# The last 64 inner MLP channels with tokens on partitions, and GpSimd yielding the shared SBUF port

## Chip, cores and metric

One core of a Trainium2 chip. The metric is the device time of one execution in microseconds (us); medians are over the runs of one kernel.

In the profile's lines PE is TensorE's matmul and PEld its weight load, DVE is VectorE, ACT ScalarE, POOL GpSimd, SP the engine that issues DMAs (a q after a name is its sequencer); L963 is line 963 of that run's kernel, so the numbers shift from run to run. SBUF is the memory that the engines work on, PSUM the one in banks into which matmuls sum.

## The reference, cut to what matters

```python
def _A_ref(x, k_cache, v_cache, wq, wo):       # attention: 32 heads of 128, 2048 queries, 2048 keys
    q = (x @ wq) ...; p = softmax(q @ k^T * Dh ** -0.5)
    return (p @ v) ... @ wo

def _B_ref(x, w1, w2, w3, w4):                 # x: 2048 tokens x 640
    h = gelu(layernorm(x) @ w1)
    hs = (four column groups of h, each shifted by +1, -1, +2, -2 tokens) @ w2
    x1 = x + hs
    h2 = gelu(layernorm(x1) @ w3) @ w4         # w3: 640 x 1728, w4: 1728 x 640
    return x1 + h2

h = layernorm(x) * (1 + ca) + sa;  x = x + ga * _A_ref(h, ...)
h = layernorm(x) * (1 + cb) + sb;  x = x + gb * _B_ref(h, ...)
```

1728 inner channels are 13 x 128 + 64. The change is about those last 64.

## The kernel before

The program is a list of operations with predicted durations; a scheduler written in Python places them in time and so fixes each engine's order of instructions, which the chip then follows with semaphores. After about 1195 us of attention comes the MLP. It works on four chunks of 512 tokens: stage A is w1, B is w2, **C the up projection (w3)**, **D the down projection (w4)**. In C channels lie on partitions: the weights are a 128x128 block of w3, the moving side is 512 tokens. The last block has 64 channels and 64 zero columns.

```python
def w3_part(ch, key):
    for f in range(NF):                        # NF = 14 blocks of 128 channels
        m = Tile(pool="T")
        for kk in range(KT):                   # KT = 5
            P.op("PE", lambda e, ...: e.matmul(m.ap, w3_ap[:, kk, f * 128:(f + 1) * 128], nT_ap[ch][:, kk, :],
                                               start=(kk == 0), stop=(kk == KT - 1)), MM(QC), ...)
        P.op("ACT", lambda e, ...: e.activation(gT_ap[:, f, :], m.ap, GELU), ...)

def w4_tile(t, key):                           # one tile of 128 tokens, two halves of 320 outputs
    ...
    for n, (mm, o, c0, c1) in enumerate(parts):
        for f in range(NF):
            P.op("PE", lambda e, ...: e.matmul(mm[:, o:o + c1 - c0], gT_ap[:, f, i * 128:(i + 1) * 128],
                                               w4_ap[f][:, c0:c1], start=(f == 0), stop=(f == NF - 1)), ...)

P.op("POOL", lambda e: e.memset(w3_ap[:, :, FF:FP], 0.0), ...)          # the zero columns
P.op("DVE", lambda e: e.memset(w4_ap[NF - 1][FL:128, :], 0.0), ...)     # and zero rows
```

The other half concerns VectorE and GpSimd. The scheduler assumes that some operations of the two ("dual": two inputs in SBUF) use a port that they share (the prediction gives the page and the traces for it), and lets neither start, in its plan, before the other's has ended. The durations it plans with are estimates:

```python
COST = {"POOL": (1600, 950), "DVE": (825, 590)}
...
x = port["POOL" if e == "DVE" else "DVE"] if o.dual else 0.0
st.append((max(r, t_eng[e], x), o.prio, o.seq, o))
...
if o.dual:
    port[e] = s + o.dur                        # planned time; no semaphore comes of it
```

Nothing makes the chip keep to the plan: if an engine is some hundred nanoseconds off, both instructions are issued at the same time after all.

Of the kernel before, what the change touches and what calls it, by code (L numbers as in the profile page):

```python
# [6 lines left out]
ACT = mybir.ActivationFunctionType  # L7
# [33 lines left out]
class Plan:  # L41
# [50 lines left out]
    def schedule(self):  # L92
# [18 lines left out]
        pe = sorted((o for o in self.ops if o.eng == "PE"), key=lambda o: (o.prio, o.seq))  # L111
        pe_i = 0
        port = {"POOL": 0.0, "DVE": 0.0}
        while len(self.all) < len(self.ops):
            best = None
            for e in self.ENG:
# [18 lines left out]
            s, o = best[0], best[3]  # L135
            e = o.eng
# [3 lines left out]
            for t in o.newps:  # L140
                b = min(free[t.pool])
# [3 lines left out]
                    o.deps.setdefault(d, False)  # L145
            o.start = s
            if o.dual:
                port[e] = s + o.dur
            t_eng[e] = s + (o.dur if o.dma or e == "PE" else max(o.dur - self.LAP.get(e, 0.0), 60.0))
            self.busy[e] += o.dur  # L150
# [129 lines left out]
def fast_path(nc, es, flag, A_x, A_k_cache, A_v_cache, A_wq, A_wo, B_w1, B_w2, B_w3, B_w4, c, w_mod, out):  # L280
    _, SQ, D = A_x.shape
    _, H, SK, DH = A_k_cache.shape
    FF = B_w3.shape[1]
    assert (SQ, D, H, SK, DH) == (2048, 640, 32, 2048, 128) and FF == 1728
    KT, NKT, HD, QC, NC = D // 128, SK // 128, D // 2, 512, SQ // 512
    NF = (FF + 127) // 128
    FL = FF - (NF - 1) * 128
    FP = NF * 128
    G4 = D // 4
    HG = 4  # L290
    NG = H // HG
# [66 lines left out]
    OT = [[T() for _ in range(4)] for _ in range(2)]  # L358
    gT_ap = OO_t[:, 0:NF * QC].rearrange("p (f q) -> p f q", f=NF)
    gT = [T() for _ in range(NF)]  # L360
    wq = [[T() for _ in range(HG)] for _ in range(2)]
    wo = [T() for _ in range(2)]
    hT = [[T() for _ in range(KT)] for _ in range(NC)]
# [12 lines left out]
    tmp = [T(t[:]) for t in tmp_t]  # L376
    rl = T(rl_t[:])
    ident, ones = T(ident_t[:]), T(ones_t[:])
    W3_OFF = 2 * KVW
    w3_ap = KV_t[:, W3_OFF:W3_OFF + KT * FP].rearrange("p (k n) -> p k n", k=KT)  # L380
    w3 = [T() for _ in range(KT)]
    W4_HI = W3_OFF + KT * FP
    NW4 = 12
    w4_ap = [KV_t[:, f * D:(f + 1) * D] for f in range(NW4)] + [KV_t[:, W4_HI + f * D:W4_HI + (f + 1) * D] for f in range(NF - NW4)]
    w4 = [T() for _ in range(3)]
    w4_of = lambda f: w4[0] if f < 6 else (w4[1] if f < NW4 else w4[2])
    assert NW4 * D <= W3_OFF and W4_HI + (NF - NW4) * D <= NKV * KVW

    MM = lambda n: n / 2.4 + 2.5
    dve = lambda n, psum=False: (n + (150 if psum else 145)) / 0.96  # L390
# [5 lines left out]
    def dma(eng, fn, kb, reads, writes, prio, need=(), after=(), over=()):  # L396
        return P.op(eng, fn, {"SP": 480, "ACT": 480, "POOL": 1000}[eng], reads, writes, prio, dma=True, kb=kb, need=need, after=after, over=over)

    def dmaT(fn, kb, reads, writes, prio, need=(), over=()):
        return P.op("SP", fn, 1270, reads, writes, prio, dma=True, kb=1.63 * kb, need=need, over=over)  # L400
# [131 lines left out]
                                              op0=ALU.subtract, op1=ALU.mult),  # L532
             445, src_t + (mvs[g][i], rs[g]), (dst_t,), prio, after=after)

    COST = {"POOL": (1600, 950), "DVE": (825, 590)}

    def tt(eng, out, a, b, op, rd, wr, prio):
        P.op(eng, lambda e: e.tensor_tensor(out=out, in0=a, in1=b, op=op), COST[eng][0], rd, wr, prio, lat=300 if eng == "POOL" else None, dual=True)  # L538
# [368 lines left out]
    for g in range(4):  # L907
        dma("SP", lambda e, g=g: e.dma_start(w_half[1][g * 32:(g + 1) * 32, 4, :], w2_rows[128:G4, g, :]), 40, (), (w2b[g],), E, over=tuple(wT[1]))
    kv = lambda *i: tuple(t for b in i for t in K[b] + [V[b]])
    for k, old in ((0, kv(2)), (1, kv(2)), (2, kv(2, 3)), (3, kv(3)), (4, kv(3, 4))):  # L910
        dma("SP", lambda e, k=k: e.dma_start(w3_ap[:, k, 0:FF], B_w3[k * 128:(k + 1) * 128, :]), 432, (), (w3[k],), E + 5 + k, over=old)
    for i, (f0, f1, old) in enumerate(((0, 6, kv(0)), (6, 12, kv(0, 1)))):
        dma("SP", lambda e, f0=f0, f1=f1: e.dma_start(KV_t[:, f0 * D:f1 * D].rearrange("p (f n) -> p f n", n=D),
                                                      B_w4[f0 * 128:f1 * 128, :].rearrange("(f p) n -> p f n", p=128)),
            960, (), (w4[i],), E + 11 + i, after=last_ot if i else (), over=old)
    dma("SP", lambda e: e.dma_start(w4_ap[NF - 2], B_w4[(NF - 2) * 128:(NF - 1) * 128, :]), 160, (), (w4[2],), E + 10, over=kv(4))
    w4b = T()
    dma("SP", lambda e: e.dma_start(w4_ap[NF - 1][0:FL, :], B_w4[(NF - 1) * 128:FF, :]), 80, (), (w4b,), E + 10, over=kv(4))

    pad, pad2 = T(), T()  # L920
    P.op("POOL", lambda e: e.memset(w3_ap[:, :, FF:FP], 0.0), 300, (), (pad,), E + 12, over=kv(2, 3, 4))
    P.op("DVE", lambda e: e.memset(w4_ap[NF - 1][FL:128, :], 0.0), 400, (), (pad2,), E + 12, slack=500.0, over=kv(4))


    DEL = [1, -1, 2, -2]
# [57 lines left out]
                    tt("DVE", v.ap, v.ap, x1[u].ap, ALU.add, (v, x1[u]), (v,), key + 100)  # L983

    def w3_part(ch, key):
        for f in range(NF):
            m = Tile(pool="T")
            for kk in range(KT):
                P.op("PE", lambda e, m=m, f=f, kk=kk: e.matmul(m.ap, w3_ap[:, kk, f * 128:(f + 1) * 128], nT_ap[ch][:, kk, :],  # L989
                                                                    start=(kk == 0), stop=(kk == KT - 1)),  # L990
                     MM(QC), (w3[kk], pad) + tuple(nT[ch]), (m,), key + f + 0.1 * kk, accum=True)
            P.op("ACT", lambda e, m=m, f=f: e.activation(gT_ap[:, f, :], m.ap, GELU),  # L992
                 act(QC), (m,), (gT[f],), key + f, over=tuple(a for b in On + OT for a in b) if ch == 0 else ())

    def w4_tile(t, key):
        i = t % 4
        b = xb[t]
        m = Tile(pool="W")
        last = t == SQ // 128 - 1
        if last:  # L1000

            m3 = Tile(pool="T")
            parts = ((m, 0, 0, HD), (m, 512, HD, 512), (m3, 0, 512, D))
        else:
            parts = ((m, 0, 0, HD), (m, 512, HD, D))
        for n, (mm, o, c0, c1) in enumerate(parts):
            for f in range(NF):
                P.op("PE", lambda e, f=f, mm=mm, o=o, c0=c0, c1=c1: e.matmul(mm[:, o:o + c1 - c0], gT_ap[:, f, i * 128:(i + 1) * 128],  # L1008
                                                                             w4_ap[f][:, c0:c1], start=(f == 0), stop=(f == NF - 1)),
                     MM(c1 - c0), (gT[f], w4_of(f), w4b, pad2), (mm,), key + n + 0.01 * f, accum=True)  # L1010
            if last:
                w, o_ = tmp[t % 2], xin[(0, 3, 1)[n]]
                P.op("DVE", lambda e, mm=mm, o=o, c0=c0, c1=c1: e.tensor_tensor(out=w[:, c0:c1], in0=mm[:, o:o + c1 - c0], in1=mod_t[5][:, c0:c1], op=ALU.mult),
                     dve(c1 - c0), (mm,) + tuple(mod[5]), (w,), key - 1000)
                P.op("DVE", lambda e, o_=o_, c0=c0, c1=c1: e.tensor_tensor(out=o_[:, c0:c1], in0=w[:, c0:c1], in1=b[:, c0:c1], op=ALU.add),
                     dve(c1 - c0), (w, b), (o_,), key)
                dma("SP", lambda e, o_=o_, c0=c0, c1=c1: e.dma_start(out2d[t * 128:(t + 1) * 128, c0:c1], o_[:, c0:c1]), 80, (o_,), (), key)
        if last:
            return
        o_ = xin[t % 4]  # L1020
        if t < SQ // 128 - 2:
            P.op("DVE", lambda e: e.tensor_tensor(out=two(b.ap), in0=wide(m), in1=two(b.ap), op=ALU.add), 825, (m, b), (b,), key - 1000)
            tt("DVE", b.ap, b.ap, mod_t[5][:], ALU.mult, (b,) + tuple(mod[5]), (b,), key)
            tt("DVE", o_.ap, b.ap, x1[t].ap, ALU.add, (b, x1[t]), (o_,), key)
        else:
            w = tmp[t % 2]
            P.op("DVE", lambda e: e.tensor_tensor(out=two(w.ap), in0=wide(m), in1=two(mod_t[5][:]), op=ALU.mult), 825, (m,) + tuple(mod[5]), (w,), key - 1000)
            tt("DVE", o_.ap, w.ap, b.ap, ALU.add, (w, b), (o_,), key)
        dma("SP", lambda e: e.dma_start(out2d[t * 128:(t + 1) * 128, :], o_.ap), 160, (o_,), (), key)
# [770 lines left out]
```

## Time and profile before

| | before |
|---|---|
| median (range) of 3 runs | 1369.59 us (1368.27 to 1372.08) |
| profiled span | 1367.0 us |
| TensorE holes, 50 to 1167 us | none |
| TensorE holes, 1167 to 1200 us | 2.04 us |
| TensorE holes, 1200 us to the end | none |

A hole is what the distance of one matmul's start to the next exceeds columns/2.4 + 2.6 ns by; how that pace was read from the chain is told in the prediction. Some matmuls have no record; a gap that is one missing matmul (216 ns at 512 columns) is not counted. Busy time by stretch (the end of attention with the first layer norms of the MLP; stages A and B with the first C; the rest). The columns are the stretch, its length, then each engine's busy us with the count of instructions, clock, DMA share and GB/s:

```profile
core 0: us, PE busy (x) PEld busy (x) DVE busy (x) ACT busy (x) POOL busy (x), PEclk, DMA share, GB/s
1165.00:1200.00 35.00, 34.17 (x318) 22.60 (x321) 29.41 (x86) 27.93 (x37) 18.46 (x17) 1.00 0.43 113
1200.00:1262.00 62.00, 61.45 (x368) 36.34 (x372) 58.22 (x168) 19.89 (x33) 0.00 (x0) 1.00 0.26 61
1262.00:1367.00 105.00, 101.53 (x632) 61.28 (x635) 50.93 (x116) 30.68 (x50) 0.00 (x0) 1.00 0.15 39
```

In the first stretch VectorE and GpSimd are both at work (29.4 and 18.5 of 35 us): of these three, only there can the port matter. Afterwards GpSimd does nothing. Now the chain over the first chunk's C, by start, length, instruction and count (L963 is B, L989 is C):

```profile
1223.52 1.36 PE f_M L963 x10
1224.88 0.05 issue
1224.93 1.03 PE f_S L989 x4
...
1238.91 1.08 PE f_O L989 x5
1239.98 1.36 PE f_S L963 x10
```

C runs from 1224.88 to 1239.98: 15.10 us for 70 matmuls, one after the other. (The 0.05 us called issue, with x4 after it, is a matmul without a record.) The place where the two engines meet is shown by two instructions on record in the prediction, at 1176.04 (GpSimd) and 1176.39 (VectorE, 1.88 us instead of some 0.88). What follows there, start and length first, with the idle time before it in brackets:

```profile
1178.19 0.48 DVE L771 TENSOR_TENSOR f_tmp<-f_M,f_mod 128x320 f32<-128x320 f32 x1
...
1180.08 1.54 POOL L538 TENSOR_TENSOR f_hT<-f_tmp,f_y 128x640 bf16<-128x640 f32 x1 [1.01 <-DVE f_rl L832]
```

L771 empties a PSUM bank that TensorE needs next; VectorE comes to it 1.0 us late, which here nothing yet waits for. GpSimd's next instruction, a memset, starts at 1178.71.

### The profile page before, as it was taken

The numbers are of one execution on the slowest core, as the hardware profiler recorded it, in microseconds if no ns is written. First come the engines' busy times: TensorE is split into PE (matmuls) and PEld (weight loads), VectorE is DVE, ScalarE is ACT, GpSimd is POOL, SyncE is SP. The second block draws the span as 40 slices with busy tenths as digits, with TensorE's granted clock in tenths as the row PEclk, the third lists the DMA queues.
The fourth block names the chain that finished last, engine by engine and source line by source line (L and its number), as shares of the span: only waits on it lengthen the run. The fifth ranks groups of instructions, "written<-read, shape, count | busy, mean of one in ns | idle before, by whom it ended". The sixth has DMA issues, their size and how long they took to land.

```text
span 1367.0 us, 29510 instructions
## 1 busy us (share of the span) xinstructions
PE 1348.4 (99%) x12778; PEld 934.7 (68%) x13012; DVE 574.7 (42%) x1442; ACT 1102.6 (81%) x1145; POOL 111.5 (8%) x97
## 2 busy tenths in 40 slices
PE   9999999999999999999999999999999999999999
PEld 5677677677667767767776766776776676655665
DVE  5554344544332332333233233233323345798553
ACT  6998888888888888888888888888888888833222
POOL 1000000000000000000000000000233337500000
PEclk9999999999999999999999999999999999999999
DMA  9742624172415221341305121522236000431110
GB/s 217 150 86 51 118 28 80 37 134 48 108 37 94 51 47 36 55 90 28 55 13 99 34 47 35 94 51 48 55 65 140 22 16 19 113 84 47 41 40 31
DMA packets 264932, 90.38 MB, mean 66 GB/s; under 512 B 245065, under 2 KB 262410, under 8 KB 264794
## 3 DMA queue, kind: packets, MB, share of 16 engines
q1 hardware_dynamic: 260826, 84.17, 30.5%
q0 software_dynamic: 672, 2.56, 0.8%
q8 instruction: 104, 1.70, 0.5%
q10 hardware_dynamic: 3296, 1.67, 0.5%
q14 instruction: 34, 0.28, 0.1%
HBM read 41.68 MB, written 2.63 MB: 32 GB/s over the span
## 4 chain that ended last, share of the span: by engine, by line
PE 97%; issue 1%; DMA 1%; DVE 1%; ACT 0%; SPq 0%; DVEq 0%
PE f_O L825 35%; PE f_S L806 29%; PE f_M L729 10%; PE f_M L760 10%; PE f_M L1008 2%; PE f_O L989 2%; PE f_S L989 2%; PE f_S L1008 2%; PE f_S L940 1%; PE f_S L963 1%; PE f_M L963 1%; PE f_O L940 1%; DMA f_W<-in_w_mod_dram 0%; DMA f_hT<-f_xn 0%; PE f_S L760 0%
## 5 line engine op out<-in xcount | busy, mean ns | idle before, releaser
L808 ACT ACTIVATE f_PQ<-f_S 128x1024 bf16<-128x1024 f32 x1024 | 1042.0, 1023 | 136.5 <-PE f_S L806 103.9
L825 PEld LDWEIGHTS f_O<-f_KV,f_PQ 128*128 128x128 bf16 x8192 | 634.9, 98 | 261.3 <-DVE f_OO L834 0.2
L825 PE MATMUL f_O<-f_KV,f_PQ 128*128 128x129 bf16 x8192 | 796.4, 220 | 8.3
L806 PE MATMUL f_S<-f_PQ,f_KV 128*128 128x512 bf16 x1831 | 650.8, 379 | 2.6 <-ACT f_PQ L808 0.5
L768 DVE TENSOR_TENSOR f_y<-f_M,f_y 128x320 f32<-128x320 f32 x192 | 94.4, 492 | 465.6 <-PE f_M L760 465.6
L760 PE MATMUL f_M<-f_wo,f_OO 128*128 128x320 bf16 x992 | 272.9, 299 | 0.0
L806 PEld LDWEIGHTS f_S<-f_PQ,f_KV 128*128 128x128 bf16 x2048 | 191.6, 98 | 13.3 <-ACT f_PQ L808 1.7
L729 PE MATMUL f_M<-f_hT,f_wq 128*128 128x512 bf16 (+1 forms) x635 | 189.1, 378 | 1.9 <-DVE f_tmp L771 0.2
L760 PEld LDWEIGHTS f_M<-f_wo,f_OO 128*128 128x128 bf16 x992 | 96.3, 98 | 28.5
L834 DVE TENSOR_TENSOR f_OO<-f_O,f_rl 128x256 bf16<-128x256 f32 x256 | 108.4, 423 | 8.3
L538 POOL TENSOR_TENSOR f_y<-f_y,f_mod 128x640 f32<-128x640 f32 x32 | 49.1, 1542 | 735.5 <-DVE f_y L768 735.4
L733 DVE CAST f_PQ<-f_M 128x512 bf16<-128x512 f32 x127 | 87.9, 692 | 49.9 <-PE f_M L729 49.6
L729 PEld LDWEIGHTS f_M<-f_hT,f_wq 128*128 128x128 bf16 x640 | 62.5, 98 | 50.6 <-DVE f_hT L595 0.8
L832 DVE RECIPROCAL f_rl<-f_O 128x2 f32<-128x2 f32 x256 | 43.6, 170 | 65.7 <-PE f_O L825 54.8
L992 ACT ACTIVATE f_OO<-f_S 128x512 bf16<-128x512 f32 x28 | 16.7, 597 | 43.6 <-PE f_S L989 43.6
L766 DVE COPY f_y<-f_M 128x320 f32<-128x320 f32 x32 | 15.7, 492 | 57.1 <-PE f_M L760 57.1
L499 DVE BATCH_NORM_STATS2 f_small<-f_y 128x6 f32<-128x320 f32 (+1 forms) x72 | 32.3, 481 | 2.5 <-DMA f_y<-in_A_x_dram 1.5
L1008 PE MATMUL f_M<-f_KV,f_OO 128*128 128x320 bf16 x224 | 31.7, 299 | 0.0
L1008 PE MATMUL f_S<-f_KV,f_OO 128*128 128x320 bf16 (+1 forms) x224 | 31.0, 296 | 0.0
L544 ACT ACTIVATE f_xn<-f_y,f_small 128x640 bf16<-128x640 f32 x10 | 9.1, 915 | 26.3 <-DVE f_small L523 21.2
L661 DVE TENSOR_REDUCE f_small<-f_tmp 128x1 f32<-128x640 f32 x20 | 16.4, 820 | 30.1 <-ACT f_PQ L808 30.1
L1008 PEld LDWEIGHTS f_M<-f_KV,f_OO 128*128 128x128 bf16 x224 | 21.9, 98 | 8.9
(151 smaller groups left out, 523.6 us busy)
## 6 DMA issues: line engine op xcount, KB each, us to landing
f_KV<-in_A_v_cache_dram SPq DMA_DIRECT2D x28, 512.0 KB, 5.0
f_wo<-in_A_wo_dram SPq DMA_DIRECT2D x8, 640.0 KB, 4.2
f_wq<-in_A_wq_dram SPq DMA_DIRECT2D x7, 640.0 KB, 4.5
f_xin<-in_A_x_dram SPq DMA_DIRECT2D x13, 320.0 KB, 3.4
out_dram<-f_xin SPq DMA_DIRECT2D x15, 160.0 KB, 1.8
f_KV<-in_B_w_dram SPq DMA_DIRECT2D x5, 432.0 KB, 3.8
f_KV<-in_A_k_cache_dram SPq DMA_TRANSPOSE x128, 2.8
f_OO<-f_OO SPq DMA_TRANSPOSE x128, 2.5
```

Source lines behind the costliest of these rows:

```text
L538: P.op(eng, lambda e: e.tensor_tensor(out=out, in0=a, in1=b, op=op), COST[eng][0], rd, wr, prio, lat=300 if eng == "POOL" else None, dual= ...
L729: P.op("PE", lambda e, i=i, kk=kk, mm=mm, a=a, z=z: e.matmul(mm[:, 0:z - a], wq_t[g % 2][:, kk, hh * 128:(hh + 1) * 128], hT_t[ch][:, kk, ...
L733: P.op("DVE", lambda e: e.tensor_copy(q.ap, m.ap), 690, (m,), (q,), s * NP - 90)
L760: P.op("PE", lambda e, m=m, qt=qt, hf=hf, hh=hh: e.matmul(m[:, 0:HD], OT_ap[gs][:, qt, hh, :], wo_t[g % 2][:, hh, hf * HD:(hf + 1) * HD], ...
L768: P.op("DVE", lambda e, m=m, yt=yt: e.tensor_tensor(out=yt.ap, in0=m[:, 0:HD], in1=yt.ap, op=ALU.add), 490, (m, yt), (yt,), s * NP - 60)
L806: P.op("PE", lambda e, sp=sp, r=r, kt=kt: e.matmul(sp[:, r * QC:(r + 1) * QC], K_ap[b][:, kt * 128:(kt + 1) * 128], q.ap, start=True, stop ...
L808: x = P.op("ACT", lambda e, sp=sp, pt=pt: e.activation(pt.ap.rearrange("p k q -> p (k q)"), sp.ap, ACT.Exp, scale=SCALE), 1021, (sp,), (pt ...
L825: ins = e.matmul(o[bk][:, w * 129:w * 129 + 129], pt[:, r, qt * 128:(qt + 1) * 128], V_ap[b][:, u, 0:129], start=(u == 0 and w == 0), stop ...
L832: P.op("DVE", lambda e, ov=ov, i0=i0: e.reciprocal(rl_t[:, i0:i0 + 2].unsqueeze(2), ov[:, 0:258].rearrange("p (u d) -> p u d", u=2)[:, :, ...
L834: evac.append(P.op("DVE", lambda e, ov=ov, i0=i0, bk=bk: e.tensor_tensor(out=On_ap[gs][:, 2 * bk:2 * bk + 2, hh, :], in0=ov[:, 0:258].rear ...
L989: P.op("PE", lambda e, m=m, f=f, kk=kk: e.matmul(m.ap, w3_ap[:, kk, f * 128:(f + 1) * 128], nT_ap[ch][:, kk, :], start=(kk == 0), stop=(kk ...
L1008: P.op("PE", lambda e, f=f, mm=mm, o=o, c0=c0, c1=c1: e.matmul(mm[:, o:o + c1 - c0], gT_ap[:, f, i * 128:(i + 1) * 128], w4_ap[f][:, c0:c1 ...
```

## The change

**Narrow tile.** For the last 64 channels the operands change places: the tokens become the weights (4 blocks of 128 tokens), the 64 columns of w3 the moving side. That is 20 short matmuls instead of 5 long ones. The result has tokens on partitions and is turned by a DMA transpose for the down projection. Two token blocks share one turned block, so the down projection uses w4's last 64 rows in an upper and a lower copy, the other half zero. A GpSimd memset of these two copies, near 1047 us, takes the place of the two memsets of before (GpSimd's at 1178.71, VectorE's at 1180.20). The narrow group is the first of its chunk.

**Port.** The scheduler gives GpSimd a real dependency (a semaphore wait) on VectorE's last dual operation where its plan has the two close together, and it plans GpSimd with shorter durations.

```diff
             if o.dual:
+                if e == "DVE":
+                    last_dual = o
+                elif last_dual is not None and s < port["DVE"] + 400.0:
+                    o.deps.setdefault(last_dual, False)
                 port[e] = s + o.dur
...
-    COST = {"POOL": (1600, 950), "DVE": (825, 590)}
+    COST = {"POOL": (1502, 858), "DVE": (825, 590)}
...
-    dma("SP", lambda e: e.dma_start(w4_ap[NF - 1][0:FL, :], B_w4[(NF - 1) * 128:FF, :]), 80, (), (w4b,), E + 10, over=kv(4))
-    P.op("POOL", lambda e: e.memset(w3_ap[:, :, FF:FP], 0.0), 300, (), (pad,), E + 12, over=kv(2, 3, 4))
-    P.op("DVE", lambda e: e.memset(w4_ap[NF - 1][FL:128, :], 0.0), 400, (), (pad2,), E + 12, slack=500.0, over=kv(4))
+    P.op("POOL", lambda e: e.memset(KV_t[:, W4Z:W4Z + 2 * D], 0.0), 1400, (), w4b, E, over=kv(2))
+    for i in range(2):
+        dma("SP", lambda e, i=i: e.dma_start(w4_ap[FN + i][i * FL:(i + 1) * FL, :], B_w4[FN * 128:FF, :]), 80, (), (w4b[i],), E + 10)
...  (w3_part; FN = 13, FL = 64)
+        m = Tile(pool="T")
+        for kk in range(KT):
+            for i in range(4):
+                c0 = (i % 2) * 128 + (i // 2) * FL
+                P.op("PE", lambda e, ...: e.matmul(m[:, c0:c0 + FL], nT_ap[ch][:, kk, i * 128:(i + 1) * 128], w3_ap[:, kk, FN * 128:FF],
+                                                   start=(kk == 0 and i == 0), stop=(kk == KT - 1), skip_group_check=True),
+                     MM(FL) + 4, (w3[kk], nT[ch][i]), (m,), key + 0.1 * kk + 0.01 * i, accum=True)
+        P.op("ACT", lambda e, m=m: e.activation(gl_ap, m[:, 0:256], GELU), ...)
+        dmaT(lambda e: e.dma_start_transpose(gT_ap[:, FN, 0:256].rearrange("p (k q) -> p k q", k=2), gl_ap), ...)
-        for f in range(NF):
+        for f in range(FN):
...  (w4_tile)
-   e.matmul(..., gT_ap[:, f, i * 128:(i + 1) * 128], w4_ap[f][:, c0:c1], ...)
+   e.matmul(..., gT_ap[:, f, (i % 2 if f == FN else i) * 128:][:, 0:128], w4_ap[f + i // 2 if f == FN else f][:, c0:c1], ...)
```

More of the change, by code (lines that the diff above doesn't have):

```diff
@@ L113, in schedule @@
         port = {"POOL": 0.0, "DVE": 0.0}
+        last_dual = None
         while len(self.all) < len(self.ops):
@@ L287, in fast_path @@
     FL = FF - (NF - 1) * 128
-    FP = NF * 128
+    FN = NF - 1
     G4 = D // 4
@@ L360, in fast_path @@
     gT = [T() for _ in range(NF)]
+    gl_ap = gT_ap[:, NF - 1, 256:512]
+    gl = T()
     wq = [[T() for _ in range(HG)] for _ in range(2)]
@@ L378, in fast_path @@
     ident, ones = T(ident_t[:]), T(ones_t[:])
-    W3_OFF = 2 * KVW
-    w3_ap = KV_t[:, W3_OFF:W3_OFF + KT * FP].rearrange("p (k n) -> p k n", k=KT)
+    W4Z = 2 * KVW
+    W3_OFF = W4Z + 2 * D
+    w3_ap = KV_t[:, W3_OFF:W3_OFF + KT * FF].rearrange("p (k n) -> p k n", k=KT)
     w3 = [T() for _ in range(KT)]
-    W4_HI = W3_OFF + KT * FP
+    W4_HI = W3_OFF + KT * FF
     NW4 = 12
-    w4_ap = [KV_t[:, f * D:(f + 1) * D] for f in range(NW4)] + [KV_t[:, W4_HI + f * D:W4_HI + (f + 1) * D] for f in range(NF - NW4)]
+    w4_ap = [KV_t[:, f * D:(f + 1) * D] for f in range(NW4)] + [KV_t[:, W4_HI + f * D:W4_HI + (f + 1) * D] for f in range(FN - NW4)] + [KV_t[:, W4Z + i * D:W4Z + (i + 1) * D] for i in range(2)]
     w4 = [T() for _ in range(3)]
     w4_of = lambda f: w4[0] if f < 6 else (w4[1] if f < NW4 else w4[2])
-    assert NW4 * D <= W3_OFF and W4_HI + (NF - NW4) * D <= NKV * KVW
+    assert NW4 * D <= W4Z and W4_HI + (FN - NW4) * D <= NKV * KVW and FL == 64
     MM = lambda n: n / 2.4 + 2.5
@@ L909, in fast_path @@
     kv = lambda *i: tuple(t for b in i for t in K[b] + [V[b]])
-    for k, old in ((0, kv(2)), (1, kv(2)), (2, kv(2, 3)), (3, kv(3)), (4, kv(3, 4))):
-        dma("SP", lambda e, k=k: e.dma_start(w3_ap[:, k, 0:FF], B_w3[k * 128:(k + 1) * 128, :]), 432, (), (w3[k],), E + 5 + k, over=old)
+    for k, old in ((0, kv(2)), (1, kv(2, 3)), (2, kv(3)), (3, kv(3, 4)), (4, kv(4))):
+        dma("SP", lambda e, k=k: e.dma_start(w3_ap[:, k, :], B_w3[k * 128:(k + 1) * 128, :]), 432, (), (w3[k],), E + 5 + k, over=old)
     for i, (f0, f1, old) in enumerate(((0, 6, kv(0)), (6, 12, kv(0, 1)))):
@@ L916, in fast_path @@
     dma("SP", lambda e: e.dma_start(w4_ap[NF - 2], B_w4[(NF - 2) * 128:(NF - 1) * 128, :]), 160, (), (w4[2],), E + 10, over=kv(4))
-    w4b = T()
-    dma("SP", lambda e: e.dma_start(w4_ap[NF - 1][0:FL, :], B_w4[(NF - 1) * 128:FF, :]), 80, (), (w4b,), E + 10, over=kv(4))
-    pad, pad2 = T(), T()
-    P.op("POOL", lambda e: e.memset(w3_ap[:, :, FF:FP], 0.0), 300, (), (pad,), E + 12, over=kv(2, 3, 4))
-    P.op("DVE", lambda e: e.memset(w4_ap[NF - 1][FL:128, :], 0.0), 400, (), (pad2,), E + 12, slack=500.0, over=kv(4))
+    w4b = T(), T()
+    P.op("POOL", lambda e: e.memset(KV_t[:, W4Z:W4Z + 2 * D], 0.0), 1400, (), w4b, E, over=kv(2))
+    for i in range(2):
+        dma("SP", lambda e, i=i: e.dma_start(w4_ap[FN + i][i * FL:(i + 1) * FL, :], B_w4[FN * 128:FF, :]), 80, (), (w4b[i],), E + 10)
     DEL = [1, -1, 2, -2]
@@ L985, in w3_part @@
     def w3_part(ch, key):
-        for f in range(NF):
+        old = tuple(a for b in On + OT for a in b) if ch == 0 else ()
+        m = Tile(pool="T")
+        for kk in range(KT):
+            for i in range(4):
+                c0 = (i % 2) * 128 + (i // 2) * FL
+                P.op("PE", lambda e, m=m, kk=kk, i=i, c0=c0: e.matmul(m[:, c0:c0 + FL], nT_ap[ch][:, kk, i * 128:(i + 1) * 128], w3_ap[:, kk, FN * 128:FF],
+                                                                     start=(kk == 0 and i == 0), stop=(kk == KT - 1), skip_group_check=True),
+                     MM(FL) + 4, (w3[kk], nT[ch][i]), (m,), key + 0.1 * kk + 0.01 * i, accum=True)
+        P.op("ACT", lambda e, m=m: e.activation(gl_ap, m[:, 0:256], GELU), act(256), (m,), (gl,), key, over=old)
+        dmaT(lambda e: e.dma_start_transpose(gT_ap[:, FN, 0:256].rearrange("p (k q) -> p k q", k=2), gl_ap), 64, (gl,), (gT[FN],), key, over=old)
+        for f in range(FN):
             m = Tile(pool="T")
@@ L990, in w3_part @@
                                                                     start=(kk == 0), stop=(kk == KT - 1)),
-                     MM(QC), (w3[kk], pad) + tuple(nT[ch]), (m,), key + f + 0.1 * kk, accum=True)
+                     MM(QC), (w3[kk],) + tuple(nT[ch]), (m,), key + 1 + f + 0.1 * kk, accum=True)
             P.op("ACT", lambda e, m=m, f=f: e.activation(gT_ap[:, f, :], m.ap, GELU),
-                 act(QC), (m,), (gT[f],), key + f, over=tuple(a for b in On + OT for a in b) if ch == 0 else ())
+                 act(QC), (m,), (gT[f],), key + 1 + f, over=old)
     def w4_tile(t, key):
@@ L1007, in w4_tile @@
             for f in range(NF):
-                P.op("PE", lambda e, f=f, mm=mm, o=o, c0=c0, c1=c1: e.matmul(mm[:, o:o + c1 - c0], gT_ap[:, f, i * 128:(i + 1) * 128],
-                                                                             w4_ap[f][:, c0:c1], start=(f == 0), stop=(f == NF - 1)),
-                     MM(c1 - c0), (gT[f], w4_of(f), w4b, pad2), (mm,), key + n + 0.01 * f, accum=True)
+                P.op("PE", lambda e, f=f, mm=mm, o=o, c0=c0, c1=c1: e.matmul(mm[:, o:o + c1 - c0], gT_ap[:, f, (i % 2 if f == FN else i) * 128:][:, 0:128],
+                                                                             w4_ap[f + i // 2 if f == FN else f][:, c0:c1], start=(f == 0), stop=(f == NF - 1)),
+                     MM(c1 - c0), (gT[f],) + ((w4b[i // 2],) if f == FN else (w4_of(f),)), (mm,), key + n + 0.01 * f, accum=True)
             if last:
```

## The prediction

> **What bounds the kernel now.** I read the page first: how busy TensorE is, then the chain that ended last.
>
> ```profile
> PE 1348.4 (99%) x12778; PEld 934.7 (68%) x13012; DVE 574.7 (42%) x1442; ACT 1102.6 (81%) x1145; POOL 111.5 (8%) x97
> ...
> PE 97%; issue 1%; DMA 1%; DVE 1%; ACT 0%; SPq 0%; DVEq 0%
> ```
>
> TensorE is on the chain for 97% of 1367.0 us, at a granted clock of 1.00. A busy share of 99% does not prove a stream without holes, because the ends of matmuls are modelled; so I took the distance from one matmul's start to the next. These are stretches of the chain in order of time (start, length, instruction, count):
>
> ```profile
> 1133.70 0.68 PE f_O L825 x12
> ...
> 1225.96 1.08 PE f_O L989 x5
> ...
> 1241.34 3.80 PE f_M L1008 x28
> ```
>
> 0.68/12 is 57 ns for 129 columns, 1.08/5 is 216 ns for 512, 3.80/28 is 136 ns for 320: columns/2.4 plus about 2.6 ns each time. At these rates the kernel's matmuls (8192 of 129 columns, 2048+640+280+100 of 512, 1024+160+448 of about 320) sum to some 1347 us. About 13 us of start and 3.2 us from the last matmul's end to the last output's landing come on top. That leaves little to win by waiting less. Waits of the weight loads from 1100 us on:
>
> ```profile
> PEld f_S L806 <- ACT f_PQ L808: 0.9, 2, 0.7
> PEld f_M L729 <- DVE f_tmp L771: 0.6, 1, 0.6
> PEld f_M L963 <- ACT f_PQ L950: 0.6, 1, 0.6
> PEld f_O L825 <- DVE f_OO L834: 0.2, 1, 0.2
> PEld f_O L825 <- ACT f_PQ L808: 0.2, 1, 0.2
> ```
>
> Taken over all pairs of matmuls, what their distance exceeds columns/2.4+2.6 ns by is 3.4 us before 50 us (the start), then nothing until 1167 us, 2.0 us from 1167 to 1200 us (the end of attention and the first MLP tile), and nothing in the 167 us of MLP after that. So the path is TensorE's own work, nearly to the nanosecond; the change can save only work it takes off TensorE, plus at most those 2.0 us.
>
> **What the Trainium skill says.** (1) "TensorE: Matmul & The Clock Gate", section "Back-to-back issue gap": a gap of N/2.4 + 2.5 ns warm, and about 60 cycles (25 ns) for 1 to 64 columns. The trace agrees at 129, 320 and 512 columns. The same section gives a slower sustained pace, about 81 ns at N=128, for streams of weight load and matmul; here such a stream runs 129 columns in 57 ns, so the measurement decides against it. For narrow matmuls with new weights each, the trace has the start of the kernel (start, length):
>
> ```profile
> 7.65 0.29 PE L465 MATMUL f_M<-f_s_bf,f_W 128*128 128x1 bf16 x6
> 7.80 0.38 PE L440 MATMUL f_S<-f_ones 128*128 128x512 bf16 x1
> ```
>
> Six one-column matmuls, each with its own 128x128 weights, take 7.65 to 7.80: 25 ns each. (2) "SBUF — State Buffer", section "Who interferes with whom": VectorE and GpSimd share a port pair as an exclusive lock for a whole instruction, and a VectorE instruction with two SBUF inputs collides with a GpSimd one that reads SBUF. The trace agrees, but has just two clear cases:
>
> ```profile
> 1176.04 1.54 POOL L538 TENSOR_TENSOR f_hT<-f_tmp,f_y 128x640 bf16<-128x640 f32 x1
> ...
> 1190.14 2.38 POOL L546 TENSOR_SCALAR f_xn<-f_y,f_small 128x640 bf16<-128x640 f32 x2 [7.01 <-ACT f_small L505]
> ```
>
> ```profile
> 1176.39 1.88 DVE L861 SCALAR_TENSOR_TENSOR f_y<-f_hT,f_small,f_mod 128x640 f32<-128x640 bf16 x1
> ...
> 1182.89 0.92 DVE L861 SCALAR_TENSOR_TENSOR f_y<-f_hT,f_small,f_mod 128x640 f32<-128x640 bf16 x1
> ```
>
> L861 takes 1.88 us under a GpSimd instruction and 0.9 alone: 1.0 us lost. At 1190 GpSimd's pair takes 2.38 instead of 1.73: 0.65 us lost.
>
> **The change, part by part.** *Removed.* Each of four chunks of 512 tokens has 14 tiles of 128 inner channels in the up projection (L989), of which the last holds 64 channels and 64 zeros. Its 5 matmuls of 512 columns go: 5 x 215.7 = 1.08 us a chunk. *Added.* 20 matmuls a chunk (4 token blocks x 5) with the tokens as weights and 64 channels as moving columns: 64/2.4 + 2.6 = 29 ns, above the 25 ns floor. 20 x 29.2 = 0.58 us. *Net.* -0.49 us a chunk, on the path because TensorE waits for nothing there: 4 x 0.49 = **-2.0 us**. The down projection (L1008) keeps all 14 matmuls per output half: the last pairs the turned block with one of two copies of the 64 weight rows, the other half zero. Nothing is saved there.
>
> *ScalarE.* The last GELU covers 256 columns instead of 512, about 0.2 us less each by the 597 ns of L992; ScalarE is idle for over 0.4 us between MLP tiles, so this is off the path.
>
> *The DMA turn.* One SBUF-to-SBUF transpose a chunk; the existing ones take some 1.3 us to issue and 2.5 to 2.7 us to land. The narrow group comes first in its chunk, and its tile is used last in each down projection, after 13 tiles x 1.08 = 14 us and 13 more matmuls (1.8 us): over ten us to spare. The queue is in order, so I compared the order of issue of both kernels. In chunk 1 the turn stands after three outputs, which in the trace issue at 1252 to 1257, before chunk 1's up projection begins at 1258; in chunk 3 also after three, issued by 1332.3, with that chunk beginning at 1333.5. No turn waits for something later than itself. Behind it some layer-norm transposes shift by about 1.3 us: those of the last chunk landed at 1268.2 and are used at 1276.0. Hidden.
>
> *Loads and memsets.* The down weights' last rows are loaded twice (80 KB more) and a GpSimd memset of 128x1280 comes near 1050 us, where GpSimd has idle gaps of 6.2 us per step. VectorE's memset (0.34 us at 1180.20, on the chain there) goes. Hidden, or a few tenths.
>
> *The port.* The order of instructions on TensorE is the same until the tail; on VectorE and GpSimd it differs from about 1130 us on. If the 1.0 us collision at 1176 goes, so may the TensorE hole just after it, 0.23 us at 1180.75 behind L834. But from 1180.9 to 1193.7 ScalarE runs 13 exponentials almost back to back, and three holes of 0.2 to 0.4 us at 1187 to 1190 are TensorE waiting for them. An earlier TensorE would wait there instead. I book **-0.2 us**, with an uncertainty of 1 us either way, because VectorE is 80% busy in these 40 us and the new order puts one L861 earlier between two evacuations that TensorE waits for.
>
> Sum: 1369.6 - 2.0 - 0.2 = **1367.4 us**, -0.16%.
>
> **The rivals.** *The narrow matmuls run at the pace of a visible weight load.* The page gives 98 ns for each; if they did not overlap, 20 x 98 = 1.96 us a chunk against 1.08 removed, +3.5 us in all: 1373. Against it speak the 25 ns of the one-column matmuls with new weights. *A part runs at some 54 ns*, as if each were 128 columns: the change is then worth nothing, 1369.5. The same lines speak against it. *The handover gets worse.* GpSimd now waits for VectorE, its tiles of the third chunk come later, VectorE (in order) waits for them, and PSUM banks that TensorE needs are freed later: +1 to +2 us, cancelling the gain, 1369. For it: two stretches of 0.2 to 0.5 us in which TensorE already waits for VectorE. Against: GpSimd idles for several us at 1162 and 1183. *All holes at the handover close*: 1365.4. Against: most are ScalarE's, whose exponentials the change leaves alone. *VectorE becomes the bound in the tail.* It is 27.5 of 30 us busy from 1200 to 1230 and 28.7 of 30 to 1260. But the first chunk's second layer norm landed at 1223.2 for a use at 1224.9, and the half microsecond saved comes after it; after 1261 VectorE idles for 12 us. I give it 5%.
>
> **Range and chances.** The work saved is nearly certain to 0.4 us, the handover to about 1 us, and the median of a few runs moves by about 1 us (before: 1368.27 to 1372.08). Together some 1.7 us either way for 8 in 10; I take 1365.2 to 1369.8. 2% is 27 us. A gain of that size is impossible, as TensorE's own sum alone is within it; a loss would need a wait that nothing shows. Faster 0.005, same 0.985, slower 0.01.
>
> **What would show it.** Right: the narrow group's 20 matmuls last 0.55 to 0.7 us from first start to the next group's first; the up projection has 260 matmuls of 512 columns instead of 280; a chunk's up projection takes about 14.6 us instead of 15.1; TensorE's waits after 1200 us stay under 0.5 us. The port step is right if no L861 and no L546 lasts much over its 0.88 us, and yet the holes from 1167 to 1200 keep more than half of their 2.0 us. Wrong: TensorE waiting for gT before a down projection (a late turn), narrow matmuls over 50 ns apart, or holes at the handover of more than 4 us.

## The result, and the profile after

| | before | after |
|---|---|---|
| median (range), same rounds | 1369.22 us (1368.27 to 1372.08), 4 runs | 1365.89 us (1365.36 to 1366.09), 4 runs |
| ratio of after to before | | 0.9972, 95% interval 0.9954 to 0.9989: same within 2% |
| profiled span | 1367.0 us | 1364.3 us |

The page of the kernel after, engines and chain, against the lines shown in the prediction:

```profile
PE 1346.9 (99%) x12838; PEld 935.6 (69%) x13072; DVE 574.9 (42%) x1441; ACT 1102.4 (81%) x1145; POOL 111.6 (8%) x97
...
PE 98%; issue 1%; DMA 0%; ACT 0%; DVE 0%; POOL 0%; DVEq 0%; POOLq 0%
```

TensorE has 60 matmuls more (4 x 15) and is 1.5 us less busy: still the whole path. The chain over the first chunk (L1000 is the narrow group, L1008 the wide tiles, L1027 stage D):

```profile
1224.87 0.58 PE f_O L1000 x20
1225.45 0.05 issue
1225.50 2.10 PE f_S L1008 x9
...
1238.40 1.08 PE f_S L1008 x5
1239.48 1.36 PE f_S L972 x10
1240.84 3.80 PE f_M L1027 x28
```

The narrow group takes 0.58 us, 29 ns a matmul. C lasts from 1224.87 to 1239.48, 14.61 us instead of 15.10. Stage D follows with its 3.80 us unchanged. That no time is lost to the turn is seen in the waits of the weight loads from 1100 us on (who, for whom; us in all, times, longest):

```profile
PEld f_S L816 <- ACT f_PQ L818: 0.9, 1, 0.9
PEld f_M L739 <- DVE f_tmp L781: 0.6, 1, 0.6
PEld f_M L972 <- ACT f_PQ L959: 0.6, 1, 0.6
PEld f_O L835 <- ACT f_PQ L818: 0.2, 1, 0.2
```

None is for the turn's tile (`f_OO`), and the wait for VectorE's L834 of before is gone. The turn itself, by duration of its issue (min/median/max in ns) and then from issue to landing:

```profile
L1004 SPq DMA_TRANSPOSE f_OO<-f_OO x4: 1169/1170/1244, 1225.9 to 1333.0; - x4
...
DMA to landing us min/median/max: 2.3/2.3/2.3
```

The stretch where the two engines meet, in the kernel after:

```profile
1173.08 0.97 DVE L871 SCALAR_TENSOR_TENSOR f_y<-f_hT,f_small,f_mod 128x640 f32<-128x640 bf16 x1
...
1174.13 1.55 POOL L548 TENSOR_TENSOR f_hT<-f_tmp,f_y 128x640 bf16<-128x640 f32 x1 [0.76 <-DVE f_y L871]
```

This L871 (L861 of before) now stands six instructions earlier in VectorE's order, GpSimd stands still for 0.76 us until it is done, and no instruction of either kind is long any more (L871 at most 0.97, L556 at most 0.88 us). TensorE's holes from 1167 to 1200 us are 1.75 us instead of 2.04: the one at 1180.75 (0.23 us) is gone; of those for ScalarE's exponentials, the two at 1187.4 and 1189.7 (0.39 and 0.20 us) have become one of 0.52. Small meetings remain: at 1188.59 VectorE's L528 takes 0.67 us under a GpSimd instruction instead of some 0.15.

To place a difference, I cut each trace at four fixed points of TensorE's order (the counts are weight loads, which are complete in all traces): **handover**, the 7000th PV load (from 0; PV is the product of softmax and values) to the last; **A+B**, the first load of stage A to the first of stage C; **C+D**, from there to the last load of stage D; **landing**, the issue of the last output to its arrival. This table holds all fourteen profiles; the experiments follow below.

| kernel | handover | A+B | C+D | landing |
|---|---|---|---|---|
| before | 171.58 | 30.42 | 138.99 | 2.27 |
| e0 before, again | 171.60 | 30.42 | 138.99 | 2.49 |
| e10 before, again | 171.60 | 30.41 | 139.00 | 2.74 |
| e2 port half alone | 171.29 | 30.42 | 138.99 | 2.37 |
| e11 port half alone, again | 171.30 | 30.42 | 138.99 | 2.08 |
| after | 171.30 | 30.42 | 137.01 | 1.56 |
| e3 after, again | 171.30 | 30.42 | 137.01 | 2.06 |
| e1 narrow half alone | 172.58 | 30.81 | 137.01 | 1.97 |
| e8 narrow half alone, again | 172.59 | 30.82 | 137.00 | 1.53 |
| e6 after, costs without rule | 171.30 | 30.42 | 137.01 | 2.14 |
| e7 after, rule without costs | 171.30 | 30.81 | 137.01 | 1.72 |
| e9 rule without costs, again | 171.30 | 30.81 | 137.01 | 1.63 |
| e4 narrow group twice | 171.29 | 30.42 | 139.34 | 2.14 |
| e5 narrow group last | 171.30 | 30.42 | 139.47 | 2.20 |

The first three columns repeat to 0.02 us from execution to execution; only the landing and the start scatter (what lies between is equal in all fourteen; the 1000th PV load lies anywhere from 154.9 to 156.9 us after the first instruction). So differences of a few tenths can be read from a trace that the times cannot resolve. Before to after: -0.28 at the handover, -1.98 in C+D, together **-2.26 us**; the remaining 0.4 us of the profiles' 2.7 is landing (-0.71) less a later start (+0.27).

### The profile page after: what moved, and what is told of

The parts are those of the page before. It is cut to its first block, busy times and chain, and to the rows that moved or that the text cites. A ratio compares the mean times of both kernels' runs of the same rounds, so it can differ in the third digit from the quotient of the medians. Undisturbed runs are those within 1.5% of the kernel's fastest.

```text
span 1364.3 us, 29631 instructions
## 1 busy us (share of the span) xinstructions
PE 1346.9 (99%) x12838; PEld 935.6 (69%) x13072; DVE 574.9 (42%) x1441; ACT 1102.4 (81%) x1145; POOL 111.6 (8%) x97
## 3 DMA queue, kind: packets, MB, share of 16 engines
q10 hardware_dynamic: 3296, 1.67, 0.5%
## 4 chain that ended last, share of the span: by engine, by line
PE 98%; issue 1%; DMA 0%; ACT 0%; DVE 0%; POOL 0%; DVEq 0%; POOLq 0%
PE f_O L835 36%; PE f_S L816 29%; PE f_M L739 10%; PE f_M L770 10%; PE f_M L1027 2%; PE f_S L1027 2%; PE f_S L1008 2%; PE f_O L1008 2%; PE f_S L972 1%; PE f_S L949 1%; PE f_O L949 1%; PE f_M L972 1%; PE f_S L450 1%; DMA f_hT<-f_xn 0%; ACT f_PQ L818 0%
## 5 line engine op out<-in xcount | busy, mean ns | idle before, releaser
L1027 PE MATMUL f_M<-f_KV,f_OO 128*128 128x320 bf16 x224 | 31.7, 299 | 0.0
L1027 PE MATMUL f_S<-f_KV,f_OO 128*128 128x320 bf16 (+1 forms) x224 | 31.0, 296 | 0.0
L1027 PEld LDWEIGHTS f_M<-f_KV,f_OO 128*128 128x128 bf16 x224 | 21.9, 98 | 8.9
L1027 PEld LDWEIGHTS f_S<-f_KV,f_OO 128*128 128x128 bf16 x224 | 21.7, 98 | 8.2
```

The lines of the kernel that those rows point to most:

```text
L1027: P.op("PE", lambda e, f=f, mm=mm, o=o, c0=c0, c1=c1: e.matmul(mm[:, o:o + c1 - c0], gT_ap[:, f, (i % 2 if f == FN else i) * 128:][:, 0:12 ...
```

## The experiments

Twelve runs of eight different kernels, all correct. My theory after the result: the narrow tile gives its 2.0 us by TensorE's own work, the port half is worth about 0.3 us. Rivals: the gain comes from the handover; the narrow matmuls cost something else than 29 ns; the turn is hidden only by luck.

### The two halves alone: e0, e1, e2, e3

The kernel before and the kernel after ran again as anchors, in the same rounds as each half alone.

e0, no edit:

> The kernel before, timed against itself, to see how large a difference may be and mean nothing. All theories: ratio 1.000, within 0.001. Theory R2 (about 1 us of the measured 3.3 us is the scatter of a few runs and of the last output's landing, and belongs to no part of the change): the landing of the last output after its issue will not be 2.27 us again as in the first profile of this kernel, but nearer to the 1.56 us of the changed kernel, and the median of this kernel over more runs will be nearer 1368.5 than 1369.6. If the landing is again about 2.3 us here and 1.6 us in the changed kernel, R2 is wrong and the changed order of the output transfers has to do with it.

e1, the kernel after without the port half:

```diff
-                if e == "DVE":
-                    last_dual = o
-                elif last_dual is not None and s < port["DVE"] + 400.0:
-                    o.deps.setdefault(last_dual, False)
-    COST = {"POOL": (1502, 858), "DVE": (825, 590)}
+    COST = {"POOL": (1600, 950), "DVE": (825, 590)}
```

> The narrow tile and its turn without the port rule and with the old cost figures in the plan. Theory W (TensorE's work): the last matmul ends 2.0 us earlier than before (1363.84), at about 1361.9, and the time falls by 2.0 us or a little more; at least two thirds of the whole gain. Rival P (the port rule brings what exceeds 2.0 us): this kernel is about 1.1 us slower than the whole change, and its holes at the handover from 1167 to 1200 us stay at 2.0 us or grow.

e2, the kernel before with those same lines the other way round (rule and new costs added, wide tile kept):

> The port rule and the new cost figures alone, with the wide zero-filled last tile as before. Theory W: -0.2 us, within 0.5, hence not to be told from zero in the time; the holes at the handover 1.7 to 2.0 us, no L861 or L546 instruction of VectorE or GpSimd much over 0.9 us. Rival P: about -1.1 us.

e3, the kernel after, no edit:

> The changed kernel again, on the same chip as the other three. Theory W with R2: -2.2 to -2.8 us against before once each has five runs, the last matmul ending 2.0 us earlier. Rival P: -3.3 us, and equal to the sum of the two parts only if the port part alone gives about -1.1.

| | median us (range, runs) | ratio to before, 95% |
|---|---|---|
| before, same rounds | 1368.96 (1368.12 to 1373.93, 11) | |
| e0 | 1368.70 (1368.3 to 1369.97, 6) | 0.9996 (0.9984 to 1.0009) |
| e1 narrow alone | 1367.55 (1366.72 to 1367.76, 6) | 0.9985 (0.9973 to 0.9997) |
| e2 port alone | 1368.78 (1367.92 to 1372.45, 6) | 0.9999 (0.9984 to 1.0014) |
| e3 both | 1366.16 (1365.18 to 1367.88, 6) | 0.9978 (0.9965 to 0.9992) |

The narrow tile alone brings its 1.98 us in C+D, yet its time is only 1.4 us lower; the port half alone is worth 0.2 us that cannot be told from nothing; both together 2.8 us. So e1 went against my theory W (2.0 us or more) and the way of rival P (1.4 us slower than the whole change, more holes), while e2 went W's way: neither theory had it. The halves do not add. The table of stretches says where: e1 is 1.28 us longer than the kernel after at the handover and 0.39 us longer in A+B. (Against before, e1's stretches sum to +1.00 + 0.39 - 1.98 = -0.59 us, 0.8 less than its medians show; its sooner landing may be part of that, see e10. The rest is not explained.) Its trace at the handover (timeline, start and length):

```profile
1176.35 1.54 POOL L542 TENSOR_TENSOR f_hT<-f_tmp,f_y 128x640 bf16<-128x640 f32 x1
1176.69 3.38 DVE L865 SCALAR_TENSOR_TENSOR f_y<-f_hT,f_small,f_mod 128x640 f32<-128x640 bf16 x1
1177.86 1.53 POOL L542 TENSOR_TENSOR f_y<-f_y,f_mod 128x640 f32<-128x640 f32 x1
1179.99 0.48 DVE L775 TENSOR_TENSOR f_tmp<-f_M,f_mod 128x320 f32<-128x320 f32 x1
...
1180.53 1.25 PE L733 MATMUL f_M<-f_hT,f_wq 128*128 128x512 bf16 x5 [0.87 <-DVE f_tmp L775]
```

and the waits of its weight loads from 1100 us on:

```profile
PEld f_M L733 <- DVE f_tmp L775: 2.0, 2, 1.4
...
PEld f_M L966 <- DVE f_y L969: 0.6, 1, 0.6
```

VectorE's L865 is recorded as starting 0.34 us after GpSimd's instruction and lasts 3.38 us instead of 0.88: it ends only after GpSimd has gone through *two* instructions back to back. L775, which empties the PSUM bank for the next query projection (L733), stands behind it in VectorE's order; TensorE waits (a hole of 1.04 us). In the kernel before the same meeting costs VectorE 1.0 us and TensorE nothing directly, because there GpSimd's second instruction was not yet ready. So the narrow half, by shifting the plan, made an old collision worse, and the port half takes it away. What in the narrow half shifted it was not tested: besides the matmuls it moves GpSimd's memset, which in the kernel before stands right behind the collision. VectorE's memset at 1180.20, which it drops, is not what the 0.28 us come from: e2 keeps that memset and has them.

One sign that e2's expectation named failed, in e2 and in e11, the same kernel: at 1189.19 a GpSimd L552 (L546 of before) takes 1.53 us instead of 0.88 and VectorE's L879 next to it 1.34 instead of 0.88. With the wide tile the port half moves this second meeting and does not remove it; no matmul waits for it.

### The price of a narrow matmul: e4

The 20 narrow matmuls of each chunk are issued twice (the result is the same, as the second pass starts the sum anew):

```diff
-        for kk in range(KT):
+        for kk in [*range(KT), *range(KT)]:
```

(The second edited line gives all 40 the same priority.)

> The changed kernel with the 20 narrow matmuls of each chunk issued twice (the second pass starts the sums anew, so the result stays right). Theory W, every nanosecond on TensorE counts at 29 ns a narrow matmul: 80 more matmuls, +2.3 us against the changed kernel, that is about -0.3 to -0.6 us against before; the stretch from the first up projection to the last matmul's start 2.3 us longer than the 137.0 us of the changed kernel. A rival in which the narrow group sits beside something else that sets the end: less than +1 us.

Measured: 1369.42 us (1367.82 to 1369.84, 5 runs), ratio 0.9998 (0.9985 to 1.0012), against 1369.01 us (9 runs) of before in these rounds. From the chain:

```profile
1226.15 1.17 PE f_O L1000 x40
```

40 matmuls take 1.17 us; C+D is 2.33 us longer than in the kernel after, 80 x 29.2 ns = 2.34 us. The price is 29 ns each and all of it is on the path. Against before that makes +0.07 us by the stretches, where I had expected -0.3 to -0.6; the times (+0.4 by the medians, -0.02% by the ratio) cannot tell these apart. (The profiled execution also began 1.3 us late, which is no effect of the edit: the table's first stretches are unchanged.)

### The turn of the last tile: e5

The narrow group goes from the first to the last place in its chunk (in words; the numbers are the priorities by which TensorE's order is set):

```diff
-   narrow group, its GELU and its turn:  key (+ 0.1 * kk + 0.01 * i)
-   wide tiles:                           key + 1 + f
+   narrow group, its GELU and its turn:  key + FN (+ 0.1 * kk + 0.01 * i)
+   wide tiles:                           key + f
```

> The changed kernel with the narrow group last in each chunk instead of first, so that the GELU (0.39 us), the turn's issue and landing (about 2.6 us) stand before the down projection that needs it after 13 x 0.136 = 1.77 us. Theory H (the turn is hidden only by its place in the order): TensorE waits some 1.3 us before the 14th matmul in the two chunks whose down projection follows at once (the third and the fourth), about nothing in the first and second; +2.6 us against the changed kernel, range 2 to 3.5. Rival: the turn is hidden anyway, +0.

Measured: 1368.58 us (1368.09 to 1369.62, 5 runs), ratio 0.9999 (0.9985 to 1.0013). Waits of the weight loads from 1200 us on:

```profile
PEld f_M L1027 <- DMA f_OO<-f_OO: 2.8, 2, 1.4
```

TensorE now waits for the turn in the last two chunks, where D follows C at once: holes of 1.25 and 1.20 us, C+D 2.46 us longer than in the kernel after. In the first two chunks a tile of stage B lies between and hides it. The whole gain is lost. So the turn is cheap because of its place in the order, not in itself: it needs more time than the 13 x 136 ns = 1.8 us of stage D that precede its use.

### Which part of the port half: e6, e7

e6 is the kernel after with the new costs but without the rule; e7 with the rule but the old costs.

```diff
e6
-                if e == "DVE":
-                    last_dual = o
-                elif last_dual is not None and s < port["DVE"] + 400.0:
-                    o.deps.setdefault(last_dual, False)
e7
-    COST = {"POOL": (1502, 858), "DVE": (825, 590)}
+    COST = {"POOL": (1600, 950), "DVE": (825, 590)}
```

> The changed kernel without the yield rule, but with the new cost figures for GpSimd in the plan. The orders of all engines come out the same as in the changed kernel; the rule adds one wait, of GpSimd's second-last normalization of the second chunk on VectorE. Theory C (the new cost figures, by reordering, are what removes the 3.4 us collision of the narrow-only kernel; the rule itself does next to nothing): equal to the changed kernel within 0.4 us, the handover 171.3 us, no long L871. Theory Y (the rule does it): about +1.3 us, as the narrow-only kernel.

> The changed kernel with the yield rule but the old cost figures. The orders are those of the narrow-only kernel; the rule adds two waits of GpSimd. Theory C: as the narrow-only kernel, about +1.3 us against the changed one, with one VectorE instruction of over 3 us near 1177 us. Theory Y: as the changed kernel.

Measured: e6 1365.98 us (1365.4 to 1367.89, 5 runs), ratio 0.9983 (0.9969 to 0.9996); e7 1366.51 us (1365.97 to 1367.74, 5 runs), ratio 0.9985 (0.9971 to 0.9998). Both have a handover of 171.30 us, as the kernel after. e6's timeline:

```profile
1172.84 0.97 DVE L865 SCALAR_TENSOR_TENSOR f_y<-f_hT,f_small,f_mod 128x640 f32<-128x640 bf16 x1
1173.09 2.13 POOL L542 TENSOR_TENSOR f_hT<-f_tmp,f_y 128x640 bf16<-128x640 f32 x1
```

e7's timeline, and its wait in A+B:

```profile
1176.43 0.87 DVE L871 SCALAR_TENSOR_TENSOR f_y<-f_hT,f_small,f_mod 128x640 f32<-128x640 bf16 x1
1177.38 1.54 POOL L548 TENSOR_TENSOR f_hT<-f_tmp,f_y 128x640 bf16<-128x640 f32 x1 [1.23 <-DVE f_y L871]
```

```profile
PEld f_M L972 <- DVE f_y L975: 0.6, 1, 0.6
```

With the new costs alone the order of instructions is that of the kernel after. The two engines still meet, but VectorE is first: GpSimd loses 0.6 us (2.13 instead of 1.54), and nobody waits for GpSimd. With the rule alone the order is that of e1, but GpSimd is held for 1.23 us. Either part prevents the harm at the handover. The 0.39 us in A+B, where TensorE waits for VectorE's L975 before stage B's second tile, comes with the order that the narrow tile gets under the old costs (e1, e7) and goes with the new ones; the kernel before, with the old costs and the wide tile, does not have it.

So e6 went theory C's way and e7 theory Y's: either part is enough, and each theory was wrong that the other part does nothing. I had compared the instruction lists of the kernels, found only one (e6) or two (e7) new waits of GpSimd, none of them at the collision, and took the rule for nearly empty. The lists show which engine is waited for, not up to which instruction; the rule had raised the value of a wait that was there before. e1 and e7 have the same instructions in the same order and differ in what three GpSimd instructions wait for: one raised wait and two new ones. That makes them the closest test of the collision: hold GpSimd back, and VectorE's 3.38 us become 0.87.

### Regular or accident: e8, e9

One instruction of 3.38 us in one profile is thin. e1 and e7 ran again, unchanged.

> The narrow tile without the rule and with the old costs, a second time, because its first profile showed one VectorE instruction of 3375 ns (the usual is 880) at the third handover between query groups, and that single event carries the port half of the explanation. Theory R (regular: the order of the instructions makes the two engines meet each time): again one scalar_tensor_tensor of over 3 us, the stretch of the last PV products across the handover again near 172.6 us instead of 171.3, the hole of 0.4 us before the second MLP stage again there, time 1367.5 (1366.9 to 1367.9). Theory A (an accident of timing in one execution): no VectorE instruction over 1.2 us, the stretch 171.3 us, and a time of 1366.2 to 1366.5.

> The rule with the old costs, a second time. Both theories: no VectorE instruction of the handovers over 1.2 us and the stretch across the third handover 171.3 us, since the rule holds GpSimd back by a wait. The hole of 0.4 us before the second MLP stage (from the first weight load of the stage to the first up projection 30.8 us instead of 30.4) comes again if it follows from the order, and is gone if it was chance. Time 1366.5 (1366.0 to 1367.0). The landing of the last output: 1.5 to 2.2 us if the kernels with the narrow tile land sooner by rule, 1.5 to 2.5 if it scatters.

Measured, in the same rounds (before 1368.63 us, 7 runs): e8 1367.28 us (1366.9 to 1367.59, 4 runs), ratio 0.9988 (0.9971 to 1.0004); e9 1366.91 us (1365.95 to 1367.74, 4 runs), ratio 0.9984 (0.9967 to 1.0001). e8's timeline:

```profile
1176.55 1.54 POOL L542 TENSOR_TENSOR f_hT<-f_tmp,f_y 128x640 bf16<-128x640 f32 x1
1176.89 3.38 DVE L865 SCALAR_TENSOR_TENSOR f_y<-f_hT,f_small,f_mod 128x640 f32<-128x640 bf16 x1
1178.06 1.53 POOL L542 TENSOR_TENSOR f_y<-f_y,f_mod 128x640 f32<-128x640 f32 x1
```

The same meeting, to 0.01 us in length, 0.20 us later as the whole execution is; handover 172.59 and A+B 30.82 again; e9 171.30 and 30.81. Theory R holds: the collision is set by the order. The two medians lie only 0.4 us apart, where the handover says 1.3; with four runs each and a start that scatters by 2 us (e9's profiled one began 1.2 us later than e8's) the times cannot show it.

### The landing of the last output: e10, e11

> The kernel before a third time, only to read how long its last output takes from issue to landing. So far the kernels with ten wide tiles took 2.27, 2.49 and 2.37 us and the nine profiles with the narrow tile 1.53 to 2.20 us. If that difference belongs to the kernels: 2.25 to 2.5 us again. If it is scatter from few samples: a value below 2.2 us is as likely as one above it. The last down-projection weight load follows the first up-projection load by 138.99 us either way.

> The port rule and the new costs with the wide tile, a second time, for the same reading: 2.25 to 2.5 us from the issue of the last output to its landing if the kernels differ, any value between 1.5 and 2.5 if it scatters. The stretch of the PV products across the third handover 171.29 us again, against 171.58 in the kernel before.

One run each: 1368.46 and 1369.46 us (before beside them 1368.88), state unknown. Landings 2.74 and 2.08 us: both lie outside the 2.25 to 2.5 us of a difference between kernels; 2.08 lies in the range of scatter, which for e10 had named no upper end. e0's landing of 2.49 had already gone against R2, while its median, 1368.70, was near the 1368.5 that R2 said. By mean, five wide profiles have 2.39 us and nine narrow ones 1.88; one kernel alone scatters by 0.5 (before: 2.27 to 2.74). Of the 45 pairs of a wide and a narrow profile in only three is the narrow one's landing the longer, so chance alone is unlikely, but no experiment shows a cause. The changed order of the outputs that e0's expectation thought of is not it: the last six are issued at the same distances in all fourteen. What varies is the last issue itself: in twelve profiles it takes 0.41 to 1.62 us, and the landing follows 1.11 or 1.12 us after its end (e2 and e11, with issues of 0.33 us, do not fit this). Whether the narrow tile has a part in those 0.5 us stays open.

## Why the prediction was right

- **What bounds the kernel.** Right: TensorE's own work. C+D repeats to 0.01 us in all profiles and moves exactly with the work put in or taken out (e4).
- **Narrow tile, -2.0 us.** Right: 0.58 us a chunk as worked out, -1.98 us in all. The rivals of 54 and 98 ns a matmul (98 ns is a weight load's duration in the profile) are excluded by e4.
- **Down projection, ScalarE, loads, memsets: nothing.** Right: no wait for any of them; stage D's tile is 3.80 us in both.
- **The turn hidden.** Right, and for the reason given, the group's place in its chunk: put last it costs 2.46 us (e5).
- **Port, -0.2 us, give or take 1.** -0.28 us at the handover. The signs named came together: no long L861 or L546, the hole at 1180.75 gone, 1.75 of 2.04 us of holes left, since most are ScalarE's. One reading was wrong: of the three holes at 1187 to 1190 that the prediction gives to exponentials, the one of 0.24 us at 1188.8 is a matmul without a record (in e0, where the record is there, it is 0.02 us). And the fear that TensorE would lose the 0.2 us again there did not come true: its two real holes went from 0.59 to 0.52 us in all. The reasoning also took the collision of the kernel *before* as what the rule removes. It did not see that the narrow tile alone would be a different schedule, with the collision at 3.38 us and two waits of TensorE worth 1.28 + 0.39 us against the kernel after. Beside the narrow tile the port half is therefore worth 1.67 us by the stretches, 1.4 by the medians of e1 and e3. The sum came out because I compared the orders of the two whole kernels, not because I knew the halves; so far it was luck.
- **The rival "the handover gets worse"** was right about the mechanism, VectorE delayed and a PSUM bank freed late, but for the narrow half alone, and the port half is its cure rather than its cause.
- **Size.** -2.2 us predicted, -2.26 by the stretches, -2.8 (e3) and -3.3 us (first result) by the medians. The predicted 1367.4 is 1.5 us above the 1365.89 measured. 0.4 us of it is the base: 1369.59 from three runs, while later medians of the same kernel are 1368.6 to 1369.2. About 0.5 may be the landing, which stays open. The rest is within the scatter of starts, and none of the three is shown to be the reason.

No version beat the kernel after: e6, without the rule, is its equal in every stretch. What remains of holes from 1167 us on waits mostly for ScalarE (0.52 and 0.17 us for exponentials, 0.44 for a GELU of stage A).

## What to carry to other kernels

In this kernel a matmul of 64 columns cost its columns and 2.6 ns even with new weights each time, so a ragged edge of 64 was worth turning round because the result's way back fitted behind other work; it did only with that group first. Before adding up the halves of a change in a kernel whose order a scheduler decides, build each half and compare the order, including the values of the waits: a half can create the very wait that the other removes. When the times scatter by more than the effect, distances between fixed instructions in the trace can still settle it.

## What the Trainium skill lacked or had wrong

- "TensorE: Matmul & The Clock Gate", section "Back-to-back issue gap": it calls columns/2.4 + 2.5 ns the gap of an isolated matmul and gives a sustained pace of about 81 ns at 128 columns and 131 ns at 512 for streams with weight loads. Such streams run at 57 ns for 129 columns and 216 ns for 512, in long runs: the formula holds, the sustained figures are too slow at one end and too fast at the other. For 64 columns its table has the floor of about 25 ns; 20 and 40 matmuls in a row with new weights each take 29 ns apiece (0.58 and 1.17 us), again the formula.
- "SBUF — State Buffer", section "Who interferes with whom": whoever issues first has the port pair for the whole instruction. The traces agree for one instruction against one (VectorE 1.88 us in the kernel before, GpSimd 2.13 us in e6). It says nothing of an owner that has a second instruction ready: there VectorE was not served in between and lost through both, 3.38 us, in two executions out of two. The other way round it was different: in e2 and e11 VectorE had a second L879 ready, yet GpSimd's L552 waited behind the first alone (1.53 us instead of 0.88), and the second L879 behind that L552 (1.34 instead of 0.88).
- "DMA: Bandwidth & Descriptors", section "DMA Transpose (X-bar)": the section has no time for a single small turn within SBUF. The one figure that was found elsewhere in the skill ("VectorE: DVE Perf Modes", section "The three transpose paths") is 1309 ns for a DMA transpose of 128x128 in bf16, without saying whether that is the issue or the landing. Here one of 128x256 elements takes 1.17 us to issue and 2.3 us from issue to landing, and where it is not hidden TensorE waits 1.2 us for it (e5).
